# Three gaps in the on-chip buffer, so that matmul operand tiles start at multiples of 512 bytes

## The chip, the core and the metric

The kernel runs on one core of a Trainium2 chip. Five engines work beside each other: TensorE (PE in the profile; its loads of the stationary operand are listed apart as PEld), VectorE (DVE), ScalarE (ACT), GpSimd (POOL) and SyncE (SP), which here only issues transfers. Operands lie in SBUF, a memory of 128 partitions; a tile takes the same byte range in each partition, and "address" below means the byte offset in a partition. Matmul results go to PSUM. The metric is the device time of one execution in microseconds (us), the median of three runs for the kernel before.

## The reference, cut to what matters

Three layers in float32 on 2 x 768 tokens: attention with 8 heads of 64, a mask and a linear bias by distance; a feed-forward layer with a softmax gate and a layer norm; a second one with a SiLU gate.

```python
# attention, per head: local window of 96 keys back, and the first 8 keys
scores = q @ k.T / 8 - slope * dist;  scores[~keep] = -1e9
x = softmax(scores) @ v                                  # -> (1536, 512)
# first layer, d_ff = 1024
h = x @ w_in;  solu = h * softmax(h)
x = layer_norm(solu) * g_ln @ w_out                      # -> (1536, 512)
# second layer, d_ff = 1536
xn = x / sqrt(mean(x * x) + 1e-6) * rms_g
out = (silu(xn @ w_gate) * (xn @ w_val)) @ w_out2        # -> (1536, 512)
```

The weights arrive as 64-bit floats, and the kernel turns their bits into 32-bit floats on the chip.

## The kernel before, in words

Tokens are worked in 12 units of 128. Precision comes from splitting: each operand of a large matmul is kept as a high and a low part (`xhi`, `xlo`; `win0`, `win1`; `lhi`, `llo`; `wout0`, `wout1`; `xgh`, `xgl`; `w2hi`, `w2lo`; `ahi`, `alo`), and each product is three matmuls (high by high, low by high, high by low) that add up in one PSUM bank. All these matmuls have one shape: a stationary operand of 128 columns, which is loaded first, and a moving operand of 512 columns. Both are 32-bit, so a weight load reads 512 bytes and a matmul 2048 bytes in every partition. There are 1872 of them, 576 in phase 1 and 1296 in phase 2:

- `up_mm` (L472, `hp`): stationary `xhi` or `xlo`, moving `win`; 12 matmuls for each half of the first layer's width.
- `down` (L557, `yp`): stationary `lhi` or `llo`, moving `wout`; 24 for each unit.
- `gate_val` (L627, `gv`): stationary a slice of `w2hi` or `w2lo`, moving `xgh` or `xgl`, the tokens of a group g of four units; 24 for each pair (f, g), where f is one of 12 slices of the second layer's width.
- `out_mm` (L651, `op`): stationary `ahi` or `alo`, moving the last third of `w2hi` or `w2lo`; 12 for each pair (f, g).

The loop of `gate_val` shows the order in which operands alternate:

```python
for k in range(KD):
    c = slice((t * KD + k) * P, (t * KD + k + 1) * P)
    for w, a in ((wh, xh), (wh, xl), (wl, xh)):
        nc.tensor.matmul(pp, w[:, c], a[:, k, :], start=(n == 0), stop=(n == 3 * KD - 1))
```

Phase 1 does attention and the first layer, unit by unit, while the first layer's weights are still being converted. Transposes (`tp`, L315, L539, L586) stand between, with an identity matrix `ident` as the other operand. Phase 2 does the second layer in three sweeps of four slices f. In a sweep g runs outside and f inside; the order on TensorE is `gate_val` of a pair, then `out_mm` of the pair before. The weights of a slice are converted shortly before their first use (`load_w2`: a transfer into `ws`; ACT scales into `wc`; three DVE steps L389, L391, L395; ACT writes `w2hi`, POOL writes `w2lo`). Slices 0 and 1 live in the pool `p_w2a`, the others take turns in the four buffers of `p_w2b`.

TensorE's order is written out by hand throughout, the other engines' order by hand in the start and by a scheduler later.

SBUF is filled from both ends: pools opened with `side="left"` are stacked upward from the constants, pools with `side="right"` downward from the top, each in the order in which they are opened, in `fast`, L673 to L718. Nothing there asks for an alignment beyond 32 bytes; where a tile starts follows from the sizes of those opened before it.

Of the kernel before, what the change touches and what calls it, by code (L numbers as in the profile page):

```python
# [12 lines left out]
F32 = mybir.dt.float32  # L13
# [9 lines left out]
P = 128  # L23
# [13 lines left out]
NLOC = 97  # L37
SWEEPS = [4, 4, 4]
MASK = 1.0e12
LEAD = 1  # L40
LAG = 2
DLAG = 3
# [75 lines left out]
class Kernel:  # L118
# [72 lines left out]
    def bias_tile(self, kind):  # L191
# [3 lines left out]
        for k, c, g in ((0, slice(2 * P, W), slice(NGLOB, NGLOB + P)), (1, slice(0, 2 * P), slice(0, NGLOB))):  # L195
# [4 lines left out]
            nc.vector.scalar_tensor_tensor(out=o, in0=r, scalar=self.nl, in1=o, op0=ALU.is_ge, op1=ALU.max)  # L200
            nc.vector.scalar_tensor_tensor(out=o, in0=o, scalar=MASK, in1=r, op0=ALU.mult, op1=ALU.add)
            nc.vector.tensor_scalar(gix[:, g], gix[:, g], self.ng, MASK, ALU.is_ge, ALU.mult)
            d = out[:, c] if c.start else out[:, P:P + NGLOB]
# [471 lines left out]
    def fast(self):  # L675
        tc, nc = self.tc, self.nc
        self.qk, self.v, self.p, self.xps, self.x = {}, {}, {}, {}, {}
        self.h, self.hst, self.ln, self.lT, self.xn = {}, {}, {}, {}, {}
        self.eps, self.gv = {}, {}
        self.sp, self.sst, self.w1, self.lps = {}, {}, {}, {}  # L680
        self.w2, self.act, self.acc, self.xg, self.pT = {}, {}, {}, {}, {}
        with ExitStack() as top:
            en = top.enter_context
            pools = {t: en(tc.tile_pool(name="ps_" + t, bufs=n, space=PSUM)) for t, n in BANKS.items()}
            self.ps = Banks(pools)
            self.p_xg = en(tc.tile_pool(name="p_xg", bufs=1, side="left"))
            self.early = (
                [self.p_xg.tile([P, 2, CW, 2], U32, tag=f"xg{t}0", name=f"ws{t}") for t in ("h", "l")],
                [self.p_xg.tile([P, 4, CW], U32, tag=f"xg{t}1", name=f"wc{t}") for t in ("h", "l")],
            )  # L690
            self.n_early = 0
            self.p_st = en(tc.tile_pool(name="p_st", bufs=DLAG + 1, side="left"))
            self.p_xn = en(tc.tile_pool(name="p_xn", bufs=2, side="left"))
            w1x = en(ExitStack())
            atx = en(ExitStack())
            we = w1x.enter_context
            ae = atx.enter_context
            self.p_w1 = we(tc.tile_pool(name="p_w1", bufs=1, side="left"))
            self.p_x = we(tc.tile_pool(name="p_x", bufs=LEAD + 1, side="left"))
            self.p_e = we(tc.tile_pool(name="p_e", bufs=LAG + 1, side="left"))  # L700
            self.p_sq = we(tc.tile_pool(name="p_sq", bufs=1, side="left"))
            self.p_l = we(tc.tile_pool(name="p_l", bufs=2, side="left"))
            self.p_bias = ae(tc.tile_pool(name="p_bias", bufs=1, side="right"))
            self.p_v = ae(tc.tile_pool(name="p_v", bufs=2, side="right"))
            self.p_qk = ae(tc.tile_pool(name="p_qk", bufs=4, side="right"))
            self.p_p = ae(tc.tile_pool(name="p_p", bufs=4, side="right"))
            self.p_pt = ae(tc.tile_pool(name="p_pt", bufs=4, side="right"))
            self.phase1()
            with tc.manual_schedule(engines={mybir.EngineType.PE}):
                atx.close()  # L710
                w2x = en(ExitStack())
                right = lambda n, b: w2x.enter_context(tc.tile_pool(name=n, bufs=b, side="right"))
                self.alloc_group(NG - 1, right("p_xg2", 1))
                self.p_ws = right("p_ws", 2)
                self.p_wc = right("p_wc", 2)
                self.p_a = right("p_a", 2)
                self.p_w2a = right("p_w2a", 2)
                self.phase2(w1x, w2x)  # L718
            w2x.close()

    def start(self):

        nc = self.nc
        self.bias_tiles()
        make_identity(nc, self.ident)
        for step in START.replace("\n", ",").split(","):
            name, *args = step.split()
            getattr(self, name)(*(int(x) if x.isdigit() else x for x in args))

    def phase1(self):  # L730
# [4 lines left out]
        with self.tc.manual_schedule(engines={E.PE}):  # L735
            for u in range(N_START, NU - LEAD):
                self.slot(u)

    def slot(self, u):

        a = u + LEAD
        s = a + 1
# [318 lines left out]
```

## Time and profile before

| what | value |
|---|---|
| median of three runs | 564.07 us (563.23 to 566.04) |
| the profiled execution's own time | 564.35 us |
| its span, first to last instruction | 562.6 us |
| TensorE busy | 535.6 us, 95% of the span |
| mean granted TensorE clock | 0.987 of full speed |
| share of TensorE in the chain that ended last | 66% |

The time contains 1.75 us outside the span. A busy share says little for TensorE here: its matmuls are pipelined, a row's duration overlaps the next matmul's, and what a matmul costs in a dense stretch is the distance from its start to the next start. A piece of the chain of waits, "x24" say, runs from the first of the merged matmuls to the start of what follows, so its length divided by the count is that distance.

### The profile page before, as it was taken

How to read it: one execution, taken by the hardware profiler on the slowest of the kernel's cores; microseconds unless marked ns; L12 is line 12 of the kernel's file. 1: busy time of each engine (PE TensorE's matmuls, PEld its weight loads, DVE VectorE, ACT ScalarE, POOL GpSimd, SP SyncE). 2: the span in 40 equal slices, each digit the busy share in tenths (PEclk: the TensorE clock that was granted, in tenths of full speed). 3: DMA queues.
4: the chain of work that ended last, by engine and by line, in shares of the span. 5: the costliest groups of instructions: out<-in, count | busy, mean ns of one | idle time of the engine just before them, and what ended most of it. 6: DMA issues, size and time to landing. Idle time of an engine off the chain costs nothing.

```text
span 562.6 us, 7639 instructions
## 1 busy us (share of the span) xinstructions
PE 535.6 (95%) x2736; PEld 425.6 (76%) x2736; DVE 333.6 (59%) x797; ACT 236.2 (42%) x557; POOL 180.9 (32%) x207
## 2 busy tenths in 40 slices
PE   4799989999999999999998999999999999999994
PEld 3466767777887788888877888888888887888883
DVE  6989999677567658965885121763213788231312
ACT  5687766574466445624434121531111443111110
POOL 4874243330332032415443111441011545111010
PEclk9979999999999999999998999999999999999998
DMA  8864611232031012422334000240000242010202
GB/s 288 258 233 164 218 52 48 91 93 78 18 94 37 16 61 75 143 82 63 125 127 136 1 0 1 75 151 0 1 0 1 80 144 76 0 76 0 76 0 82
DMA packets 16670, 45.93 MB, mean 82 GB/s; under 512 B 1904, under 2 KB 2928, under 8 KB 16624
## 3 DMA queue, kind: packets, MB, share of 16 engines
q1 hardware_dynamic: 16624, 45.36, 24.2%
q8 instruction: 23, 0.38, 0.3%
q14 instruction: 23, 0.19, 0.1%
HBM read 42.21 MB, written 3.15 MB: 81 GB/s over the span
## 4 chain that ended last, share of the span: by engine, by line
PE 66%; DVE 21%; POOL 4%; ACT 4%; issue 2%; DMA 2%; SPq 0%; POOLq 0%; ACTq 0%; DVEq 0%
PE gv L627 27%; PE op L651 14%; PE yp L557 11%; PE hp L472 9%; DVE p L277 3%; DVE wc L391 2%; POOL p L299 2%; DVE e L504 2%; PE tp L315 2%; DVE wc L395 2%; DVE wc L389 2%; PE xps L337 1%; DMA ws<-in_w 1%; DVE hst L480 1%; ACT wc L217 1%
## 5 line engine op out<-in xcount | busy, mean ns | idle before, releaser
L627 PE MATMUL gv<-xgh,w2hi 128*128 128x512 f32 x288 | 114.0, 396 | 0.0
L627 PE MATMUL gv<-xgl,w2hi 128*128 128x512 f32 x288 | 113.7, 395 | 0.0
L627 PE MATMUL gv<-xgh,w2lo 128*128 128x512 f32 x288 | 113.7, 395 | 0.0
L223 POOL TENSOR_TENSOR alo<-th,ahi 128x512 fp32r<-128x512 f32 x36 | 48.0, 1332 | 175.9 <-ACT ahi L222 175.9
L299 POOL TENSOR_SCALAR p<-p,ast 128x256 f32<-128x256 f32 (+1 forms) x96 | 57.9, 619 | 103.2 <-DVE ast L281 67.6
L614 DVE SCALAR_TENSOR_TENSOR th<-th,gv 128x512 f32<-128x512 f32 x36 | 24.7, 685 | 102.9 <-ACT th L613 102.9
L223 POOL TENSOR_TENSOR w2lo<-wc,w2hi 128x512 fp32r<-128x512 f32 x36 | 49.3, 1372 | 63.2 <-ACT w2hi L222 63.2
L472 PE MATMUL hp<-win,xhi 128*128 128x512 f32 x192 | 66.0, 407 | 0.7 <-ACT xhi L217 0.7
L627 PEld LDWEIGHTS gv<-xgl,w2hi 128*128 128x128 f32 x288 | 54.3, 188 | 12.8
L627 PEld LDWEIGHTS gv<-xgh,w2lo 128*128 128x128 f32 x288 | 54.2, 188 | 12.9
L627 PEld LDWEIGHTS gv<-xgh,w2hi 128*128 128x128 f32 x288 | 54.3, 188 | 12.7
L557 PE MATMUL yp<-wout,lhi 128*128 128x512 f32 x192 | 61.0, 398 | 0.3 <-DVE wout L455 0.3
L651 PE MATMUL op<-w2hi,alo 128*128 128x512 f32 x144 | 57.5, 400 | 1.5 <-POOL alo L223 1.5
L222 ACT ACTIVATE ahi<-th 128x512 fp32r<-128x512 f32 x36 | 22.7, 631 | 85.6 <-DVE th L615 85.6
L651 PE MATMUL op<-w2hi,ahi 128*128 128x512 f32 x144 | 57.0, 396 | 0.9 <-ACT ahi L222 0.9
L613 ACT ACTIVATE th<-gv 128x512 f32<-128x512 f32 x36 | 21.3, 592 | 85.1 <-PE gv L627 85.1
L651 PE MATMUL op<-w2lo,ahi 128*128 128x512 f32 x144 | 56.9, 395 | 0.0
L288 ACT ACTIVATE p<-p,ast 128x256 f32<-128x256 f32 (+1 forms) x96 | 45.9, 480 | 6.5 <-DVE ast L281 3.2
L615 DVE SCALAR_TENSOR_TENSOR th<-th,gv 128x512 f32<-128x512 f32 x36 | 24.6, 684 | 32.8 <-PE gv L627 32.6
L472 PEld LDWEIGHTS hp<-win,xhi 128*128 128x128 f32 x192 | 37.1, 193 | 9.2 <-ACT xhi L217 1.4
L557 PEld LDWEIGHTS yp<-wout,lhi 128*128 128x128 f32 x192 | 34.9, 188 | 7.3 <-DVE wout L455 0.8
L472 PE MATMUL hp<-win,xlo 128*128 128x512 f32 x96 | 38.7, 403 | 0.5 <-DVE xlo L355 0.5
(118 smaller groups left out, 911.7 us busy)
## 6 DMA issues: line engine op xcount, KB each, us to landing
ws<-in_w SPq DMA_DIRECT2D x36, 512.0 KB, 3.3
qk<-in_qk SPq DMA_DIRECT2D x20, 384.0 KB, 4.0
v<-in_v SPq DMA_DIRECT2D x10, 512.0 KB, 4.0
out_dram<-acc SPq DMA_DIRECT2D x12, 256.0 KB, 3.1
wsh<-in_w_in SPq DMA_DIRECT2D x4, 512.0 KB, 5.5
wsl<-in_w_in SPq DMA_DIRECT2D x4, 512.0 KB, 6.0
wsh<-in_w_out SPq DMA_DIRECT2D x4, 512.0 KB, 3.9
wsl<-in_w_out SPq DMA_DIRECT2D x4, 512.0 KB, 4.5
```

The costliest lines, as they stand in the source:

```text
L222: self.nc.scalar.activation(out=hi, in_=src, func=AF.Copy)
L223: lo_eng.tensor_tensor(lo, src, f32(hi), ALU.subtract)
L277: nc.vector.tensor_tensor_reduce(pt[:, i, 0:W], sp[h2][:, pl, :], bias[:, 4 * hh + i, :], 1.0, -3.0e38, ALU.add, ALU.max, st[:, 0, i:i + 1],)
L288: self.nc.scalar.activation(out=pt[:, i, 0:W], in_=pt[:, i, 0:W], func=AF.Exp, scale=0.125, bias=st[:, 1, i:i + 1], accum_out=st[:, 2, i:i ...
L299: nc.gpsimd.tensor_scalar(pt[:, i, 0:W], pt[:, i, 0:W], st[:, 3, i:i + 1], 0.0, ALU.mult, ALU.add)
L472: nc.tensor.matmul(hp, a[:, k, :], self.win[w][:, k, c], start=(n == 0), stop=(n == len(mms) - 1))
L557: nc.tensor.matmul(yp, a[:, k, :], self.wout[w][:, k, :], start=(k == 0 and n == 0), stop=(k == KF - 1 and n == 2),)
L613: nc.scalar.activation(out=a, in_=g, func=AF.Tanh, scale=0.5)
L614: nc.vector.scalar_tensor_tensor(out=a, in0=a, scalar=1.0, in1=g, op0=ALU.add, op1=ALU.mult)
L615: nc.vector.scalar_tensor_tensor(out=a, in0=a, scalar=0.5, in1=v, op0=ALU.mult, op1=ALU.mult)
L627: nc.tensor.matmul(pp, w[:, c], a[:, k, :], start=(n == 0), stop=(n == 3 * KD - 1))
L651: nc.tensor.matmul(self.ops[t], a[:, c], w[:, c0], start=(first and n == 0), stop=(last and n == 2))
```

## The change

Three pads are allocated: 96 bytes at the left, ahead of `p_xg`; 384 bytes at the left, ahead of `p_xn`; 480 bytes at the right, ahead of `p_bias`. No instruction reads or writes them.

```diff
+PAD_G, PAD_X, PAD_R = 96, 384, 480
...
             self.ps = Banks(pools)
+            self.pad(top, "left", PAD_G)
             self.p_xg = en(tc.tile_pool(name="p_xg", bufs=1, side="left"))
...
             self.p_st = en(tc.tile_pool(name="p_st", bufs=DLAG + 1, side="left"))
+            self.pad(top, "left", PAD_X)
             self.p_xn = en(tc.tile_pool(name="p_xn", bufs=2, side="left"))
...
             self.p_l = we(tc.tile_pool(name="p_l", bufs=2, side="left"))
+            self.pad(top, "right", PAD_R)
             self.p_bias = ae(tc.tile_pool(name="p_bias", bufs=1, side="right"))
...
+    def pad(self, stack, side, n):
+
+        pool = stack.enter_context(self.tc.tile_pool(name=f"pad_{side}{n}", bufs=1, side=side))
+        pool.tile([P, n // 4], F32, name=f"pad_{side}{n}")
```

The built program has the same instructions in the same order with the same waits on every engine; only addresses differ. Left tiles move up by 96 or 480 bytes, right tiles down by 480. The remainders of the start addresses modulo 512, as the built program allocates them (slices within a tile start a multiple of 512 further, so they have the tile's remainder):

| tiles | before | after |
|---|---|---|
| `xgh`, `xgl` of groups 0 and 1 (and the early weight staging in their place) | 416 | 0 |
| `xgh`, `xgl` of group 2 | 480 | 0 |
| `w2hi`, `w2lo` of slices 0 and 1 (`p_w2a`) | 480 | 0 |
| `w2hi`, `w2lo` of slices 2 to 11 (`p_w2b`) | 32 | 0 |
| `th`, `ahi`, `alo`, `ws`, `wc` | 480 | 0 |
| `win`, `wout`, `xhi`, `xlo`, `lhi`, `llo`, `e`, `xn`, `acc` | 32 | 0 |
| `qk`, `v`, `p`, `pT`, bias | 480 | 0 |
| `ident` | 128 | 128 |

All the remainders of before but that of `ident` are 32 above a multiple of 64.

## Rows read from the trace of the kernel before

**Rows 1.** The page: busy time by engine; granted TensorE clock in 40 slices

```profile
PE 535.6 (95%) x2736; PEld 425.6 (76%) x2736; DVE 333.6 (59%) x797; ACT 236.2 (42%) x557; POOL 180.9 (32%) x207
...
PEclk9979999999999999999998999999999999999998
```

**Rows 2.** The page: shares of the chain that ended last, by engine

```profile
PE 66%; DVE 21%; POOL 4%; ACT 4%; issue 2%; DMA 2%; SPq 0%; POOLq 0%; ACTq 0%; DVEq 0%
```

**Rows 3.** Chain of waits in time, phase 1: start us, us, what

```profile
158.03 5.48 PE yp L557 x24
163.50 2.73 PE hp L472 x12
166.23 0.87 PE tp L315 x8
...
220.74 0.87 PE tp L539 x8
```

**Rows 4.** Chain of waits in time, phase 2

```profile
318.28 5.46 PE gv L627 x24
323.75 2.76 PE op L651 x12
326.51 5.49 PE gv L627 x24
332.00 2.72 PE op L651 x12
334.72 5.60 PE gv L627 x24
...
351.43 5.59 PE gv L627 x24
...
469.41 5.57 PE gv L627 x24
```

**Rows 5.** Timeline of PE, 297 to 301.6 us: start us, us, what

```profile
299.12 0.63 PE L651 MATMUL op<-w2lo,ahi 128*128 128x512 f32 x1
...
300.82 0.63 PE L651 MATMUL op<-w2hi,alo 128*128 128x512 f32 x1
```

**Rows 6.** Busy time by stretch of phase 2: length, each engine, clock, DMA share, GB/s

```profile
297.48:301.45 3.97, 3.97 (x11) 3.15 (x12) 2.60 (x5) 1.83 (x3) 1.19 (x1) 0.60 0.37 123
301.45:435.10 133.65, 133.65 (x577) 108.29 (x577) 46.86 (x66) 29.31 (x49) 30.78 (x23) 1.00 0.10 32
435.10:466.84 31.74, 31.20 (x136) 24.82 (x134) 25.50 (x32) 13.64 (x24) 16.64 (x13) 1.00 0.35 116
466.84:562.60 95.76, 88.68 (x382) 71.75 (x382) 29.86 (x43) 16.28 (x27) 18.24 (x14) 0.97 0.11 40
```

**Rows 7.** Chain of waits in time: conversion of second-layer weights and what ends it

```profile
257.20 2.51 POOL w2lo L223 x2
...
295.90 1.54 POOL alo L223
297.48 3.97 PE op L651 x10
...
465.50 1.29 POOL alo L223
```

**Rows 8.** Timeline of all engines, 430 to 440 us: ACT's wait

```profile
435.14 1.15 ACT L222 ACTIVATE w2hi<-wc 128x512 fp32r<-128x512 f32 x2 [1.41 <-PE op L651]
```

**Rows 9.** Stretch 74.7 to 242.6 us, lines L472 and L557 alone: PE, PEld

```profile
74.70:242.60 167.90, 47.19 (x192) 35.46 (x192) 1.00 0.22 70
...
74.70:242.60 167.90, 62.90 (x258) 47.25 (x258) 1.00 0.22 70
```

**Rows 10.** Groups of instructions by line: busy us, mean ns | idle before, releaser

```profile
L223 DVE TENSOR_TENSOR llo<-tp,lhi 128x512 fp32r<-128x512 f32 x24 | 15.5, 681 | 0.0
...
L223 DVE TENSOR_TENSOR xgl<-tp,xgh 128x512 fp32r<-128x512 f32 x12 | 8.2, 684 | 3.5 <-ACT xgh L222 3.5
```

## Prediction

> **What bounds the kernel now.** I read the page's totals first: TensorE is busy 95% of the span at nearly full clock [rows 1]. That alone proves nothing, so the chain of waits came second: 66% of it is TensorE, 21% DVE [rows 2]. Third came the chain in order of time. In phase 1 every unit is a run of TensorE pieces, 24 `yp`, 12 `hp`, 8 transposes, 12 `hp` [rows 3]; in phase 2, outside two stretches, it is `gv` x24 and `op` x12 in turn with nothing between [rows 4]. The two stretches are the conversions of second-layer weights: from 257.2 us the chain is on POOL, DVE and ACT until POOL delivers `alo` and TensorE goes on at 297.48, and again until 465.5 + 1.29 us [rows 7]. The stretch table says the same: from 301.45 to 435.10 TensorE is busy for all of 133.65 us, while the others are busy a third of it or less [rows 6]. There, and from 466.84 on, a matmul that starts sooner ends the kernel sooner.
>
> The reader is to look next at how long one matmul of 512 columns takes, by the chain's pieces, beside the table of remainders. The same 24 `gv` take 5.46 and 5.49 us at 318 and 326 us, and 5.60, 5.59 and 5.57 us at 334, 351 and 469 us [rows 4]: 227.5 and 228.8 ns for one against 233.3, 232.9 and 232.1. The first two are slices 0 and 1 with group 2: weights at 480 modulo 512, moving tiles at 480. The piece at 334 us has the same moving tiles, but slice 2, whose weights are at 32. The pieces at 351 and 469 us have 416 and 32. In phase 1, where weights and moving tiles are both at 32, 24 `yp` take 5.48 us and 12 `hp` 2.73: 228.3 and 227.5 ns [rows 3]. And 12 `op` take 2.72 us (226.7 ns) with both at 480, at 332 us, but 2.76 (230 ns) with 32 and 480, at 323 us [rows 4]. So the quick pieces are those in which the stationary and the moving operand have the same remainder, whatever it is (32 or 480). No other engine is in it: TensorE waited for nothing in these pieces.
>
> **The change part by part.** It adds and removes no instruction and no wait, so the whole effect is in durations. It gives every pair of operands of `gv` and `op` what `yp`, `hp` and a few `gv` have already: equal remainders.
>
> The sum, for the profiled execution. Stretch 301.45 to 435.10: 577 matmuls in 133.65 us are 231.6 ns each [rows 6]. At 226.7 (the `op` piece of 2.72 us [rows 4]) they take 130.8: 2.8 us less; at 227.5 (the `gv` piece of 5.46) 131.3: 2.4 less. Stretch from 466.84: 382 matmuls in 88.68 us of TensorE, 232.1 each [rows 6]; of this some 0.2 us is the last one's pipeline tail, so 231.7, and at 226.7 to 227.5 the gain is 1.9 to 1.6 us. I take the settled rate in both, since I read the first matmuls of a run as the slower ones and these runs are long, less 0.1 for settling after each of the two stalls: 2.7 + 1.8 = 4.5 us.
>
> What does not come through. From 257.20 to 297.48 the chain is the conversion, and TensorE arrives early and waits [rows 7]; faster matmuls there only make that wait longer. The same holds from 435.10 to 466.84: that conversion starts when ACT has waited 1.41 us for the last `op` on the old slice [rows 8], so it moves forward with TensorE, but its length of some 31 us is its own. What it hides of TensorE is 136 matmuls by 5 ns, 0.7 us. The stretch at the lower clock after the first stall (0.60 mean [rows 6]) follows from that wait and stays; matmuls started 299.12 to 300.82 in four steps of 425 ns there [rows 5], against 227 to 233 elsewhere. In phase 1 the remainders were equal already, so it gains nothing by this.
>
> Other durations that could move with addresses: DVE's subtraction of a low part takes 681 ns into tiles at 32 and 684 into tiles at 416 and 480 [rows 10], so I put compute engines at 0. Eight transposes take 0.87 us whether they read `p` (480) or `e` (32), with `ident` at 128 [rows 3]: 0. Transfers into shifted tiles have no row to compare. They are 2% of the chain [rows 2], 11 us; a tenth of that either way, an estimate, is 1.1 us, and I take 0. If the conversion chain (31.7 and 40.3 us) were 1% slower or faster, 0.7 us.
>
> 564.35 - 4.5 = 559.85 us for the profiled execution, which stood 0.28 above the median of 564.07: **559.5 us**. Own range of this case 557.5 to 561.5.
>
> [...]
>
> **The rivals.**
>
> [...]
>
> *Nothing changes, about 564.* The quick pieces are quick for a reason other than the remainder: distance between tiles, or what ran just before. Against it stand five sorts of pairs that sort by equality alone; for it, that every tile keeps its neighbours and the evidence is only pieces that are 2% apart. Or TensorE's gain returns as a longer wait for `alo` at 465 us.
>
> *Slower: zero breaks what settles.* The quick rate may be a pattern in which weight load and matmul read the same 512-byte frame in step, and starting both at the very beginning of a frame may make them meet each time. Then phase 1 loses what it has: 450 matmuls go from 228 to 233.3 ns, 2.4 us, and phase 2 gains nothing: 566.5. If both phases went to 236 ns, 3.6 + 959 by 4.4 ns, 4.2: 572. It decides from the point where `yp` x24 takes more than 5.6 us. For it: no pair of before starts at a multiple of 64. Against: of the remainders seen, equality was all that mattered.
>
> **How the numbers follow.** Forecast 0.55, floor falls too 0.20, nothing 0.13, slower 0.12. About 0.5% (2.8 us) is what a measurement here can tell from no change. Faster by more, below 561.25: most of the forecast (0.49) and the floor (0.20), 0.69. Within: the weak edge of the forecast and the no-change case, 0.18. Slower: 0.13. The range for 8 in 10 goes from 545, inside the second half of the floor's case, to 566, short of most of the slower one.
>
> **What would show it.** `gv` x24 in the chain at 5.46 us or a little less in all three sweeps; `op` x12 at 2.72; `yp` x24 still at 5.45 to 5.48; the stretch of 577 matmuls near 131 us; TensorE's two waits for `alo` longer by about 0.7 us each; durations on DVE, ACT and POOL unchanged. I am wrong if `gv` stays at 5.6 or `yp` changes. `yp` at 5.3 or less is the floor's case, above 5.6 the slower one.

## The result, and the profile after

The changed kernel takes 559.16 us (median of 6 runs, 558.12 to 559.82), against 563.89 us (median of 6) for the kernel before: a ratio of 0.9912, 95% interval 0.9885 to 0.9939. The forecast was 559.5 us.

The profiled execution of the change took 558.12 us, its span is 556.3 us. These are lines of its page, as in [rows 1, 2]; line numbers are one higher than before, because the change adds a line at the top.

```profile
PE 527.8 (95%) x2736; PEld 423.9 (76%) x2736; DVE 333.3 (60%) x797; ACT 236.3 (42%) x557; POOL 180.4 (32%) x207
...
PE 65%; DVE 22%; POOL 4%; ACT 4%; issue 2%; DMA 1%; POOLq 0%; ACTq 0%; DVEq 0%; SPq 0%
```

Only TensorE's busy time moved, by 7.8 us (that of its weight loads, PEld, by 1.7); the other engines' is the same to 0.5 us. The chain of waits of the changed kernel in order of time (start us, us, what), first where it answers to [rows 3], then to [rows 4 and 7]:

```profile
158.55 5.46 PE yp L558 x24
164.01 2.72 PE hp L473 x12
166.73 0.87 PE tp L316 x8
...
296.10 1.54 POOL alo L224
297.68 2.57 PE op L652 x10
300.25 5.44 PE gv L628 x24
305.69 2.72 PE op L652 x12
...
332.89 5.44 PE gv L628 x24
...
349.21 5.44 PE gv L628 x24
...
461.28 1.28 POOL alo L224
462.60 2.56 PE op L652 x10
465.16 5.44 PE gv L628 x24
```

The pieces of phase 1 are as they were. They start 0.5 us later; a second profiled execution of the same program, below, starts them 1.9 us later still, so 0.5 us can't be put down to the pads. From 300.25 us on, every `gv` piece is 5.44 us, where before they were 5.46 to 5.60 (the first, behind the stall, 5.77), and every `op` piece of 12 is 2.72 or 2.73: 226.7 ns for each matmul. The pieces no longer differ by group or slice. Busy time by stretch (length, PE, PEld, DVE, ACT, POOL, clock, DMA share, GB/s), cut at the points that answer to those of [rows 6]:

```profile
297.68:300.25 2.57, 2.57 (x11) 2.15 (x12) 1.72 (x3) 1.47 (x3) 1.19 (x1) 1.00 0.55 188
300.25:430.82 130.57, 130.57 (x577) 108.12 (x577) 47.89 (x68) 29.54 (x50) 30.58 (x23) 1.00 0.10 33
430.82:462.60 31.78, 30.43 (x134) 24.71 (x134) 25.48 (x32) 14.04 (x24) 16.62 (x13) 1.00 0.35 116
462.60:556.35 93.75, 86.90 (x382) 71.57 (x382) 29.79 (x43) 15.93 (x27) 18.17 (x14) 0.98 0.11 41
```

The two profiled executions differ by 6.2 us. The stretch of 577 matmuls gave 133.65 - 130.57 = 3.1 of it, the last stretch of 382 gave 1.8 (88.68 to 86.90 us of TensorE), the tail behind it 0.2, and the conversion between the two stretches nothing (31.74 and 31.78). TensorE resumes 0.2 us later at the first stall. The remaining 1.4 us are the 10 `op` after that stall: 3.97 us at a mean granted clock of 0.60 before, 2.57 at 1.00 here. That part is not the change's: in a second profiled execution of the same program, below, they took 3.82 us at 0.63, and in the kernel with the right pad alone, below, 2.58 us. Some 0.2 of the 3.1 us belong with it, an estimate from two pieces of before: the first `gv` behind the stall, whose first step is still 430 ns, took 5.77 us, the next of the same remainders 5.57. That leaves 2.9 us to the pads.

```profile
301.45 5.77 PE gv L627 x24
...
309.96 5.57 PE gv L627 x24
```

The gain that TensorE makes inside the conversions came back as waiting. TensorE's own waits, before and after (us in total, times, longest):

```profile
PE op L651 <- POOL alo L223: 1.5, 2, 0.9
PE op L651 <- ACT ahi L222: 0.9, 1, 0.9
```

```profile
PE op L652 <- POOL alo L224: 2.3, 2, 1.3
...
PE op L652 <- ACT ahi L223: 1.3, 1, 1.3
```

These waits are 1.2 us longer in all.

### The profile page after: what moved, and what is told of

Read it like the earlier page. It is cut to its first block, busy times and chain, and to the rows that moved or that the text cites. A ratio compares the mean times of both kernels' runs of the same rounds, so it can differ in the third digit from the quotient of the medians.

```text
span 556.3 us, 7639 instructions
## 1 busy us (share of the span) xinstructions
PE 527.8 (95%) x2736; PEld 423.9 (76%) x2736; DVE 333.3 (60%) x797; ACT 236.3 (42%) x557; POOL 180.4 (32%) x207
## 4 chain that ended last, share of the span: by engine, by line
PE 65%; DVE 22%; POOL 4%; ACT 4%; issue 2%; DMA 1%; POOLq 0%; ACTq 0%; DVEq 0%; SPq 0%
PE gv L628 26%; PE op L652 14%; PE yp L558 11%; PE hp L473 9%; DVE p L278 3%; DVE wc L392 3%; POOL p L300 2%; DVE e L505 2%; DVE wc L396 2%; DVE wc L390 2%; PE tp L316 2%; PE xps L338 1%; ACT wc L218 1%; DVE hst L481 1%; PE tp L587 1%
## 5 line engine op out<-in xcount | busy, mean ns | idle before, releaser
L628 PE MATMUL gv<-xgh,w2hi 128*128 128x512 f32 x288 | 112.2, 390 | 0.0
L628 PE MATMUL gv<-xgl,w2hi 128*128 128x512 f32 x288 | 112.1, 389 | 0.0
L628 PE MATMUL gv<-xgh,w2lo 128*128 128x512 f32 x288 | 112.0, 389 | 0.0
```

## The experiments

Theory A: the distance between the start of the stationary operand and that of the moving operand, modulo 512 bytes, sets the rate, and equal remainders give the quick one. Theory B: a start at a multiple of 64 or of 512 gives it. The change makes both true at once, so it can't tell them apart.

Four kernels ran on one chip in five rounds, 6 to 12 runs of each, with the kernel before beside them.

**The change again.** No edit.

> The changed kernel once more, beside the three others on one chip. Both theories: 0.991 of before, 559 us; gv x24 in the chain 5.44 us, op x12 2.72, yp x24 5.44 to 5.48.

Measured: 559.53 us, ratio 0.9919 (0.9890 to 0.9947). 25 of 27 `gv` pieces of the chain are 5.44 us; the other two are 5.49, between pieces of phase 1, and 5.81 behind the first stall. Its stretch of 10 `op` after the first stall, columns as above:

```profile
299.50:303.32 3.82, 3.82 (x11) 3.06 (x12) 3.15 (x5) 1.73 (x3) 1.20 (x1) 0.63 0.34 124
```

**All tiles at 32.**

```diff
-PAD_G, PAD_X, PAD_R = 96, 384, 480
+PAD_G, PAD_X, PAD_R = 128, 384, 448
```

> Every operand tile at 32 modulo 512 instead of 0, ident as before. Theory A (only equality of the remainders of weights and moving operand counts): as the change, 0.991, 559 us, gv x24 5.44 us, op x12 2.72. Theory B (a start at a multiple of 64 or of 512 counts): as before, 0.999 to 1.0, 563 to 564 us, gv x24 5.6.

Measured: 559.81 us, ratio 0.9925 (0.9896 to 0.9954). The chain of this kernel:

```profile
159.24 5.49 PE yp L558 x24
...
326.67 5.44 PE gv L628 x24
332.11 2.72 PE op L652 x12
```

No operand tile of these matmuls lies at a multiple of 64, and the gain is there as in the run above. Theory B is out as the cause of the gain.

**Phase 2 unequal, all at multiples of 64.**

```diff
-PAD_G, PAD_X, PAD_R = 96, 384, 480
+PAD_G, PAD_X, PAD_R = 32, 448, 480
...
+                self.pad(w2x, "right", 64)
                 self.alloc_group(NG - 1, right("p_xg2", 1))
+                self.pad(w2x, "right", 448)
```

> As the change, but xgh and xgl of all groups at 448 modulo 512, weights and all else at 0, so that everything is a multiple of 64 and gv's pairs are unequal. Theory A: gv x24 back at 5.58 to 5.61 us; op, whose pairs are equal, 2.72 to 2.77 since it must settle anew after each gv; 625 gv on the path by 5.8 ns are 3.6 us, op 0.3: 563 us, 0.998. Theory B: as the change, 559 us, gv x24 5.44.

Measured: 563.11 us, ratio 0.9985 (0.9964 to 1.0006), so the gain is gone. Its chain:

```profile
320.08 5.60 PE gv L628 x24
325.68 2.74 PE op L652 x12
328.42 5.60 PE gv L628 x24
```

All three groups show 5.60 (the first piece behind the stall, 5.78). The `op` pieces, equal pairs, take 2.74 and not 2.72 behind an unequal `gv`.

**Phase 1 unequal.**

```diff
+            self.pad(w1x, "left", 64)
             self.p_x = we(tc.tile_pool(name="p_x", bufs=LEAD + 1, side="left"))
```

> As the change, but xhi, xlo, e, lhi, llo at 64 modulo 512 against win and wout at 0: phase 1's pairs, equal before and after, are made unequal, phase 2 keeps what the change gave. Theory A: yp x24 5.58 to 5.61 us, hp x12 2.78 to 2.80, 450 matmuls by 5 to 6 ns are 2.3 to 2.7 us: 561.6 us, 0.996; gv stays at 5.44. Theory B: as the change, 559 us, yp x24 5.44 to 5.48.

Measured: 561.87 us, ratio 0.9955 (0.9937 to 0.9973). Its chain:

```profile
160.19 5.61 PE yp L558 x24
165.80 2.80 PE hp L473 x12
...
321.08 5.44 PE gv L628 x24
```

What phase 1 had without anybody's asking is taken away by 64 bytes: the 450 matmuls of [rows 9] by 5 ns, 2.3 us of 561.87 - 559.53.

The next four ran once each. Their single times spread with the run (the one of before beside them was 566.84 us), so the pieces of the chain decide, not the times.

**Distances, first three.** The pads between the tiles of `p_xg` and around `p_xg2` set each group's place:

```diff
-PAD_G, PAD_X, PAD_R = 96, 384, 480
+PAD_G, PAD_M, PAD_X, PAD_R = 352, 384, 256, 480
...
+            self.pad(top, "left", PAD_M, self.p_xg)
...
+                self.pad(w2x, "right", 192)
                 self.alloc_group(NG - 1, right("p_xg2", 1))
+                self.pad(w2x, "right", 320)
```

> As the change, but xgh and xgl of group 0 at 256, of group 1 at 128, of group 2 at 320 modulo 512, weights at 0. It asks for the modulus. Theory A with 512: all three groups' gv x24 at 5.5 to 5.62 us. With 256: group 0 at 5.44, the others at 5.5 to 5.62. With 128: groups 0 and 1 at 5.44. Theory B: all at 5.44. Whole time 560 to 564 us by A.

Measured: 562.48 us. One piece each of group 2 (320), group 0 (256) and group 1 (128), in the chain's order:

```profile
343.65 5.51 PE gv L628 x24
349.16 2.77 PE op L652 x12
351.93 5.44 PE gv L628 x24
...
384.57 5.59 PE gv L628 x24
```

A distance of 256 gives 5.44 us, as 0 does, and 128 gives 5.59: in this run equality counts modulo 256, not modulo the 512 of the change and of theory A as it was put.

**Distances, next three.** The same edit with `PAD_G, PAD_M, PAD_X` at 128, 160, 192 and 448 and 64 at the right.

> As the change, but xgh and xgl of group 0 at 32, of group 1 at 192, of group 2 at 64 modulo 512, weights at 0. Theory A: all three groups' gv x24 at 5.5 to 5.62 us, unless an offset is found that settles as well. Theory B with 64: group 0 at 5.6, groups 1 and 2 at 5.44.

Measured: 565.33 us. Group 2 (64), then group 0 (32); group 1 (192) has 5.60 too:

```profile
345.18 5.51 PE gv L628 x24
...
353.46 5.60 PE gv L628 x24
```

64 gives 5.51, as 320 did, which is 64 modulo 256: the second pair that agrees modulo 256. This distance costs about half, 0.07 us of a piece against 0.16 at 32 and 192.

**The right pad alone.**

```diff
-            self.pad(top, "left", PAD_G)
...
-            self.pad(top, "left", PAD_X)
```

> The pad at the right alone: right tiles at 0, left tiles as before (416 and 32). Theory A: equal pairs are gv of group 2 with slices 0 and 1 and op of these slices, as before, so nothing is gained: 563 to 564 us, other gv x24 5.55 to 5.61. Theory B: op, whose stationary tiles are now at 0 but whose moving tiles are at 32, and gv are in between; no clear gain either.

Measured: 563.86 us. `gv` as expected, but `op`, whose moving tiles lie 32 above its stationary ones now, is slower than before:

```profile
358.81 5.59 PE gv L628 x24
364.40 2.80 PE op L652 x12
```

**The left pads alone.**

```diff
-            self.pad(top, "right", PAD_R)
```

> The two pads at the left alone: left tiles at 0, right tiles at 480. Theory A: gv of groups 0 and 1 with slices 2 to 11 is equal and goes to 5.44 us, group 2 with these slices stays at 5.6, op (0 and 480) at 2.75 to 2.77; some 16 of 26 gv pieces on the path by 0.14 us are 2.2 us: 561.5 to 562 us. A theory by distance between tiles would leave gv of groups 0 and 1 where it was, since p_w2b and these tiles moved by 480 and 96 only.

Measured: 562.32 us. Slice 2 with group 2 (unequal), then a later slice with group 0 (equal), and the `op` behind it:

```profile
334.36 5.59 PE gv L628 x24
...
359.35 5.45 PE gv L628 x24
364.80 2.79 PE op L652 x12
```

`gv` came out as expected. `op` did not: 2.79, where 2.75 to 2.77 was expected. That range was copied from before, where `op`'s moving tiles lay 64 above the stationary ones; here it is 32. The two distances differ, as the ladder shows, and what the pads at the left give to `gv` they take back in part from `op`.

**Distances, the last three.** The same edit with 320, 384, 288 and 352 and 160 at the right.

> As the change, but xgh and xgl of group 0 at 224, of group 1 at 96, of group 2 at 160 modulo 512, weights at 0: the three distances modulo 256 that no run has shown. So far moving minus weights of 0 settles at 227 ns, 64 at 229.6, and 32, 128 and 192 at 233. If only equality modulo 256 settles, all three groups are at 229 to 234 ns (gv x24 5.5 to 5.62 us); if some distance does better than equality, one of them is under 5.44.

Measured: 562.74 us, one run. Group 2 (160), group 0 (224) and group 1 (96), which has 5.61 and once 5.62:

```profile
333.33 5.62 PE gv L628 x24
...
358.37 5.60 PE gv L628 x24
...
383.41 5.61 PE gv L628 x24
```

None of the eight distances in steps of 32 does better than the 5.44 us of equality.

**Half of each weight load.** In `gate_val`:

```diff
-                    nc.tensor.matmul(pp, w[:, c], a[:, k, :], start=(n == 0), stop=(n == 3 * KD - 1))
+                    m = slice(c.start, c.start + (128 if n in (0, 3 * KD - 1) else 64))
+                    nc.tensor.matmul(
+                        pp[0:m.stop - m.start, :], w[:, m], a[:, k, :], start=(n == 0), stop=(n == 3 * KD - 1)
+                    )
```

The 213 ns in the expectation are an estimate: half of the 425 ns from start to start that [rows 5] shows of the kernel before, since the granted clock from 299.12 to 300.82 us was 0.50 of full. No run shows a matmul of 512 columns in that time at full clock. The 14 ns are the rest of 227.

> As the change, but in gate_val the ten middle matmuls of each twelve load and use only the first 64 of the 128 stationary columns (so half of the second layer's products are left out); the moving operand stays at 512 columns. It asks what the 14 ns over the columns' own 213 ns are. If they come from weight loads and matmuls reading at once, half the load leaves some 220 ns and gv x24 goes to 5.28 to 5.32 us. If they belong to the matmul alone, gv x24 stays at 5.44.

Measured: 559.88 us, one run. Neither number came:

```profile
324.91 5.51 PE gv L629 x24
330.42 2.73 PE op L655 x12
333.15 5.51 PE gv L629 x24
```

With smaller loads the matmuls came out slower, 229.6 ns against 226.7, at equal remainders and with the same moving reads. So the excess over the estimated 213 ns did not shrink here, it grew from 14 to 17. But the edit changes more than the load: each such matmul also writes 64 partitions of its result instead of 128, and two in twelve keep 128. Which of these slowed it is not shown, and what the excess is stays open.

**One pad fewer.** All tiles at 480, five rounds:

```diff
-PAD_G, PAD_X, PAD_R = 96, 384, 480
+PAD_G, PAD_X = 64, 384
...
-            self.pad(top, "right", PAD_R)
```

> No pad at the right; at the left 64 bytes ahead of p_xg and 384 ahead of p_xn, so that every operand tile lies at 480 modulo 512 and one pad is saved. Theory A (equality alone): as the change, 0.991, 559 us, gv x24 5.44 us, op x12 2.72. Theory B (a multiple of 64 or 512): 0.999, 563 to 564 us, gv x24 5.6.

Measured: 559.92 us, ratio 0.9932 (0.9907 to 0.9956).

```profile
328.47 5.44 PE gv L628 x24
333.91 2.72 PE op L652 x12
```

The same rate at a third common remainder, for 448 bytes instead of 960. It does not beat the change; no run did.

## Why the prediction was right

*What bounds the kernel.* Right: what the pads gained came in the two stretches in which TensorE alone is the chain.

*The cause.* Right: equality of the remainders, shown from both sides. Common remainders 0, 32 and 480 give 5.44 us; unequal ones at multiples of 64 give 5.60 in phase 2 and take 24 `yp` of phase 1 from at most 5.49 to at least 5.59. Reading it from the kernel before was possible because that kernel held five sorts of pairs, two of them equal by chance, all of one shape and three of them (`gv`) of one line of code. Why an equal start is quicker no run shows.

*The modulus.* The table of before could not tell 512 from 256: its unequal pairs had distances of 64, 384 and 448, none of them a multiple of 256. The runs say 256: `gv` x24 took 5.44 us at a distance of 256 as at 0, 5.51 at 320 as at 64, and 5.59 at 128. The forecast did not suffer, since what is equal modulo 512 is equal modulo 256.

*The sizes.* First stretch: 2.7 us forecast, 3.1 measured, of which some 0.2 belong to the clock. Last stretch: 1.8 and 1.8 (the 231.7 ns put down for it are 231.6 by its own figures, which leaves the sum as it is). For settling I took off 0.1 in each, and the first `gv` piece behind each stall (at 300.25 and 465.16 us) is at 5.44 already. The waits for `alo` and `ahi` were to grow by 0.7 us at each stall, and grew by 1.2 us together. What was put at zero, other engines, transposes and transfers, moved by less than 0.3 us (tail and resume point). The low clock behind the first stall was put down to TensorE's wait there and was to stay. In the profiled execution it did not come (mean granted clock 1.00 over the 10 `op`, against 0.60 before) though these waits had grown; what lowers it is not shown. With the full clock there that execution was 1.6 us shorter than the pads alone would have made it, 558.12 against 559.85 forecast. It is no part of the gain: the medians differ by 4.7 us here and by 4.2, 3.9 and 3.7 in the five-round runs of the change, of all tiles at 32 and of one pad fewer, around the 4.5 forecast.

*Where the operands lie.* With the moving tiles and the instructions unchanged, moving the stationary tiles of phase 1 by 64 bytes takes 24 `yp` from 5.46 to 5.61 us (the pieces at 158.55 and 160.19 us); with the weights unchanged, moving `xgh` and `xgl` takes a `gv` matmul from 226.7 to 233.3 ns. Moved together, to a common 32 or 480, the operands of 24 `gv` kept 5.44 us: in these runs only the distance between the two counted. How this comes about no run shows, and whether a matmul's own load counts or the next one's none tells apart, since all loads of a piece have one remainder.

*The rivals.* The floor, the rate of the quick pieces, did not fall. That case (its chance of 0.20, `yp` at 5.3 us or less, the 545 us at which the range begins) needs matmuls well below 227 ns at zero remainders, and no run shows any: there 24 `gv` take 5.44 us, 226.7 ns each, as they do at common remainders of 32 and 480, and 24 `yp` took 5.44 to 5.49 us. "Nothing changes" fell with both comparisons of the change (0.9912 and 0.9919). The slower case did not come: 24 `yp` kept 5.44 to 5.49 us at zero, and no run shows a frame of 512 bytes.

## What to carry to other kernels

Where TensorE is the chain with 32-bit operands, divide a piece of the chain by its count and compare pieces of one shape: a spread of 2 or 3% between them that no wait explains can be the operands' place in SBUF, as it was here (24 `gv` took 5.44 to 5.62 us, away from the stalls). Try stationary and moving tiles that start at the same remainder modulo 256 bytes. Here that gave the quickest piece, and which remainder did not matter (0, 32 and 480 were tried); 960 bytes of padding did it, or 448, and in phase 1 of the kernel before the order of the pools gave it by itself. A gain on the bounding engine counts only in the stretches where that engine is the chain: here 1.2 us of it went back into waits for another engine.

## What the runs showed of the hardware that was not expected

How a matmul of 512 columns went in these runs, with 128 x 128 loads, against the distance of the moving operand's start from the stationary one's, modulo 256 (`gv` x24 divided by 24; 0 in the change, the others in the three runs of distances; 0 and 64 were run at 256 and 320 too, with the same times):

| distance | 0 | 32 | 64 | 96 | 128 | 160 | 192 | 224 |
|---|---|---|---|---|---|---|---|---|
| `gv` x24, us | 5.44 | 5.60 | 5.51 | 5.61 to 5.62 | 5.59 | 5.62 | 5.60 | 5.60 |
| ns each | 226.7 | 233.3 | 229.6 | 233.8 to 234.2 | 232.9 | 234.2 | 233.3 | 233.3 |

An equal pair started slower behind an unequal one: 12 `op` took 2.74 us behind the unequal `gv` of 5.60 (phase 2 unequal), 2.72 behind equal ones (the change). In the kernel before, the equal `gv` piece behind an unequal `op` starts with six steps of 230 ns on average, then come 18 of 226.7 (timeline of PE: start us, us, what):

```profile
318.12 0.39 PE L627 MATMUL gv<-xgh,w2hi 128*128 128x512 f32 x1
...
319.50 0.39 PE L627 MATMUL gv<-xgh,w2hi 128*128 128x512 f32 x1
...
323.58 0.40 PE L651 MATMUL op<-w2hi,ahi 128*128 128x512 f32 x1
```

The distance did not fix the unequal rate to the last half per cent: in the kernel before, pairs at 416 and 32 took 5.59 and 5.60 us from 351.43 to 418.36 us, but 5.57 in the six pieces from 469.41 us on, behind the second stall [rows 4]. What sets this is not shown. And `gv` with 64 columns loaded took 5.51 us against 5.44 with 128, so the smaller load was no gain in that run.
